# Attention block on one core: four-head score batches in a ring of three bank pairs, and one score bank in seven exponentiated on VectorE

## The chip, the cores and the metric

One core of one Trainium2 chip. The metric is device time in microseconds (us) of the core, the median over the runs named; lower is better. The kernel before takes 1316.6 us (two runs, 1308.5 and 1324.7). Every run also reports the mean clock that TensorE was granted, as a share of its full clock; runs more than 1.5% above the fastest of the same kernel are called slow and are left out of ratios.

## The reference

A transformer block in bf16 for 2048 tokens of width 640: multi-query attention (32 query heads of 20 dimensions, one head of keys and values), then a gated GELU feed-forward part of width 1536.

```python
def block(x, wq, wk, wv, wo, w_gate, w_up, w_down):       # x: 1 x 2048 x 640
    n = layernorm(x)
    q = (n @ wq).reshape(B, S, 32, 20).transpose(0, 2, 1, 3)
    k, v = n @ wk, n @ wv                                  # one head of 20, shared
    scores = einsum("bhqd,bkd->bhqk", q, k) * 20 ** -0.5
    o = einsum("bhqk,bkd->bhqd", softmax(scores), v)
    h = x + o.transpose(0, 2, 1, 3).reshape(B, S, 640) @ wo
    m = layernorm(h)
    return h + (gelu(m @ w_gate, approximate=True) * (m @ w_up)) @ w_down
```

The costly thing is the softmax: 32 x 2048 x 2048 exponentials. As 128 partitions that is 2048 PSUM banks of 128x512 fp32 scores.

## The kernel before

The heads have only 20 dimensions, so four of them lie on top of each other in the 128 rows of the TensorE array, 32 rows each. A "unit" is 128 keys x 512 columns (four head groups x 128 queries). Scores of two heads are computed into a pair of banks by two matmuls over 32 rows each, ScalarE exponentiates the pair (128x1024) into SBUF, and once four heads are done, four matmuls of 32 columns each multiply by the values. Keys lie in the partitions, so no transposition is needed; a column of ones in `v_ext` gives the softmax denominators.

The kernel divides PSUM into eight banks. Before: two pairs for scores, one bank for the value products, three for everything else (projections, feed-forward).

```python
A_BANKS = [0, 2]          # pairs: banks 0,1 and 2,3
V_BANKS = [4]
M_BANKS = [5, 6, 7]
...
def qk_source(e_name):
    ...
    nu = 2                                    # two heads in a batch
    tile = Tile(pA)                           # one bank pair
    ...
    def fn(e):
        for i, u in enumerate(range(u0, u0 + nu)):
            s, r, t, hf, kt = unit_info(u)
            ins = e.matmul(
                bank(A_BANKS[tile.slot] + i), kT4[32 * r:32 * r + 32, kt * P:(kt + 1) * P],
                qT[32 * r:32 * r + 32, (t // 4) % 2, 4 * hf:4 * hf + 4, (t % 4) * P:(t % 4) * P + P],
                start=True, stop=True, tile_position=(32 * r, 0))
        return ins
    o = Op("pe", fn, 300, deps, prio=-1000 + 0 * u0, acq=[tile], name=f"qk{u0}")
    ...
        ex = pl.add(Op("act", lambda e: e.activation(pa_sb[:, pt.slot, :], bank(A_BANKS[tile.slot], 2), ACT.Exp, scale=SM),
                       928, (o_,), prio=-1000, acq=[pt], name=f"exp{u0}"))
...
def make_pv(s):
    ...
        for r in range(4):
            _, pt, off = us[r]
            ins = e.matmul(bank(V_BANKS[vt.slot])[32 * r:32 * r + 32, :], v_ext[:, kt, :], pa_sb[:, pt.slot, off:off + 512],
                           start=(kt == 0), stop=(kt == NKT - 1), tile_position=(0, 32 * r))
```

The kernel is not written as loops. Each operation gets a planned duration and priority; a planner lays them out in time as the program is built and so fixes the order in which every engine gets its instructions. One that is late can then hold up those that stand behind it on its engine (in g2 below, 28.3 us of ScalarE).

The softmax here doesn't subtract the row's maximum and nothing guards it: scores larger than these inputs give would overflow.

## Time and profile before

| kernel before | value |
|---|---|
| time | 1316.6 us |
| mean granted clock of TensorE | 0.63 |
| busy: TensorE / ScalarE / VectorE / GpSimd | 88% / 77% / 17% / 20% |
| ScalarE waits for score matmuls | 248.0 us, 290 times |
| first exponential starts / last one ends | 16.25 / 1276.4 us |

The totals, the clock row, the chain of waits and the group of exponentials stand in the prediction below, with their reading. In the middle part, from 400 to 1260 us, the view by stretches says (columns: stretch and length, then busy time and count of TensorE, weight loads, VectorE, ScalarE and GpSimd, the granted clock, DMA share, GB/s):

```profile
400.00:1260.00 860.00, 774.93 (x3930) 219.55 (x3969) 121.44 (x257) 687.06 (x729) 189.06 (x204) 0.62 0.05 12
```

ScalarE is busy for 687 of 860 us here, at a clock of 0.62.

### The profile page before, as it was taken

The numbers are of one execution on the slowest core, as the hardware profiler recorded it, in microseconds if no ns is written. First come the engines' busy times: TensorE is split into PE (matmuls) and PEld (weight loads), VectorE is DVE, ScalarE is ACT, GpSimd is POOL, SyncE is SP. The second block draws the span as 40 slices with busy tenths as digits, with TensorE's granted clock in tenths as the row PEclk, the third lists the DMA queues.
The fourth block names the chain that finished last, engine by engine and source line by source line (L and its number), as shares of the span: only waits on it lengthen the run. The fifth ranks groups of instructions, "written<-read, shape, count | busy, mean of one in ns | idle before, by whom it ended". The sixth has DMA issues, their size and how long they took to land.

```text
span 1315.5 us, 14670 instructions
## 1 busy us (share of the span) xinstructions
PE 1160.0 (88%) x6129; PEld 342.5 (26%) x6188; DVE 220.3 (17%) x529; ACT 1018.0 (77%) x1081; POOL 266.0 (20%) x294
## 2 busy tenths in 40 slices
PE   5788888999997889989998888989999888999997
PEld 3311112222222222222222222222222222222245
DVE  6401010111112111021101211111010111111115
ACT  5598978788789876788767997688877898677861
POOL 3000001222013310223103221023211222013241
PEclk7755566655569765575556876576556766555669
DMA  5620000000000000000000000000000000000000
GB/s 147 146 103 14 9 14 9 9 15 2 18 14 14 9 9 11 14 14 9 9 13 13 14 9 14 19 1 13 9 14 19 10 14 1 18 14 9 14 0 21
DMA packets 47273, 27.33 MB, mean 21 GB/s; under 512 B 34408, under 2 KB 41960, under 8 KB 47208
## 3 DMA queue, kind: packets, MB, share of 16 engines
q1 hardware_dynamic: 47208, 26.40, 7.8%
q8 instruction: 48, 0.79, 0.2%
q14 instruction: 17, 0.14, 0.0%
HBM read 18.34 MB, written 2.88 MB: 16 GB/s over the span
## 4 chain that ended last, share of the span: by engine, by line
PE 53%; ACT 34%; DMA 5%; SPq 2%; DVE 2%; issue 2%; POOL 1%
ACT pa_sb L688 33%; PE ps L673 18%; PE ps L867 12%; PE ps L721 9%; PE ps L923 7%; PE ps L795 4%; PE ps L590 3%; SPq L410 2%; DMA rL<-lscr 1%; DMA lcol<-osb 1%; DMA lscr<-lrec 1%; POOL onT L769 1%; ACT th L890 1%; DMA xnT<-xn 1%; POOL sq L883 1%
## 5 line engine op out<-in xcount | busy, mean ns | idle before, releaser
L688 ACT ACTIVATE pa_sb<-ps 128x1024 bf16<-128x1024 f32 x1024 | 988.0, 1031 | 254.4 <-PE ps L673 248.0
L673 PE MATMUL ps<-qT,kT 32*128 32x512 bf16 x2048 | 545.2, 537 | 100.0 <-ACT pa_sb L688 87.7
L721 PE MATMUL ps<-pa_sb,v_ext 128*32 128x512 bf16 x2048 | 281.5, 541 | 3.5 <-ACT pa_sb L688 3.5
L673 PEld LDWEIGHTS ps<-qT,kT 32*128 32x128 bf16 x2048 | 102.3, 97 | 532.9 <-ACT pa_sb L688 413.8
L769 POOL TENSOR_TENSOR onT<-osb,rL 128x512 bf16<-128x512 f32 x31 | 39.2, 1264 | 555.2 <-DMA rL<-lscr 555.2
L867 PE MATMUL ps<-xnT,wg 128*128 128x256 bf16 (+1 forms) x540 | 113.0, 371 | 0.0
L923 PE MATMUL ps<-wd,hh 128*128 128x128 bf16 (+1 forms) x370 | 105.8, 419 | 5.7 <-issue 3.3
L721 PEld LDWEIGHTS ps<-pa_sb,v_ext 128*32 128x32 bf16 x2048 | 55.4, 98 | 192.7 <-issue 183.3
L883 POOL TENSOR_TENSOR sq<-gs 128x512 bf16<-128x512 bf16 x45 | 46.7, 1038 | 265.8 <-DVE gs L422 265.8
L867 PE MATMUL ps<-xnT,wu 128*128 128x256 bf16 (+1 forms) x540 | 94.5, 326 | 3.4 <-POOL sq L883 3.4
L422 DVE CAST gs<-ps 128x512 bf16<-128x512 f32 x45 | 31.1, 691 | 324.4 <-PE ps L867 324.4
L795 PE MATMUL ps<-wo_pad,onT 128*128 128x128 bf16 (+1 forms) x231 | 61.7, 386 | 16.5 <-POOL onT L769 8.4
L867 PEld LDWEIGHTS ps<-xnT,wg 128*128 128x128 bf16 x540 | 57.0, 128 | 53.2 <-issue 37.5
L867 PEld LDWEIGHTS ps<-xnT,wu 128*128 128x128 bf16 x540 | 51.3, 116 | 45.3 <-issue 24.4
L590 PE MATMUL ps<-xnT,wq_pad 128*128 128x512 bf16 (+1 forms) x140 | 51.2, 478 | 4.9 <-issue 4.9
L895 POOL TENSOR_TENSOR hg<-th,gs 128x512 bf16<-128x512 bf16 x45 | 52.1, 1159 | 3.7
L887 POOL TENSOR_TENSOR zz<-sq,gs 128x512 bf16<-128x512 bf16 x45 | 51.8, 1151 | 3.6
L904 DVE TENSOR_TENSOR hh<-hg,ps 128x512 bf16<-128x512 bf16 x48 | 32.3, 673 | 103.7 <-POOL hg L895 98.0
L893 POOL TENSOR_SCALAR th<-th 128x512 bf16<-128x512 bf16 x45 | 27.8, 617 | 86.6 <-ACT th L890 86.6
L744 DVE COPY osb<-ps 128x512 f32<-128x512 f32 x32 | 22.1, 691 | 133.7 <-PE ps L721 133.7
L923 PEld LDWEIGHTS ps<-wd,hh 128*128 128x128 bf16 x384 | 30.1, 116 | 53.8 <-issue 43.7
L422 DVE CAST qT<-ps 128x512 bf16<-128x512 f32 (+1 forms) x33 | 21.5, 654 | 126.1 <-PE ps L590 124.0
(66 smaller groups left out, 280.3 us busy)
## 6 DMA issues: line engine op xcount, KB each, us to landing
rL<-lscr SPq DMA_DIRECT2D x124, 64.0 KB, 2.0
out_dram<-xh SPq DMA_DIRECT2D x16, 160.0 KB, 1.8
lcol<-osb SPq DMA_DIRECT2D x124, 2.0 KB, 1.7
xh<-in_A_x_dram SPq DMA_DIRECT2D x6, 320.0 KB, 6.3
wg<-in_B_w_gate_dram SPq DMA_DIRECT2D x1, 1920.0 KB, 7.6
wu<-in_B_w_up_dram SPq DMA_DIRECT2D x1, 1920.0 KB, 13.1
wd<-in_B_w_down_dram SPq DMA_DIRECT2D x1, 1920.0 KB, 17.8
wq_st<-in_A_wq_dram SPq DMA_DIRECT2D x2, 400.0 KB, 4.4
```

The source lines that it names most:

```text
L422: return e.tensor_copy(o_ap(), i_ap())
L590: ins = e.matmul(bank(M_BANKS[mt.slot])[:, 0:n], wq_pad[:, c, g, :], xnT[:, c, tok], start=(c == 0), stop=(c == ND - 1))
L673: ins = e.matmul(bank(A_BANKS[tile.slot] + i), kT4[32 * r:32 * r + 32, kt * P:(kt + 1) * P], qT[32 * r:32 * r + 32, (t // 4) % 2, 4 * hf:4 ...
L688: ex = pl.add(Op("act", lambda e: e.activation(pa_sb[:, pt.slot, :], bank(A_BANKS[tile.slot], 2), ACT.Exp, scale=SM), 928, (o_,), prio=-10 ...
L721: ins = e.matmul(bank(V_BANKS[vt.slot])[32 * r:32 * r + 32, :], v_ext[:, kt, :], pa_sb[:, pt.slot, off:off + 512], start=(kt == 0), stop=( ...
L769: mu = op("pool", lambda e: e.tensor_tensor(onT[:, nt_.slot, 4 * hf:4 * hf + 4, :].rearrange("p g n -> p (g n)"), osb[:, ot.slot, :], rL[: ...
L795: ins = e.matmul(bank(M_BANKS[tl_.slot])[:, 0:c1 - c0], onT[:, nt_.slot, g, :], wo_pad[:, g, c0:c1], start=(g == 0), stop=(g == NG - 1))
L867: ins = e.matmul(bank(M_BANKS[tl_.slot])[:, j * n:(j + 1) * n], w[:, c, fc * P:(fc + 1) * P], xnT[:, c, tok], start=(c == 0), stop=(c == N ...
L883: a1 = op(pE, (lambda gt, st_: lambda e: e.tensor_tensor(sq[:, st_.slot, :], gs[:, gt.slot, :], gs[:, gt.slot, :], ALU.mult))(gt, st_), tt ...
L887: a3 = op(pE, (lambda gt, st_, zt: lambda e: e.tensor_tensor(zz[:, zt.slot, :], sq[:, st_.slot, :], gs[:, gt.slot, :], ALU.mult))(gt, st_, ...
L895: a6 = op(pE, (lambda gt, tt, ht_: lambda e: e.tensor_tensor(hg[:, ht_.slot, :], th[:, tt.slot, :], gs[:, gt.slot, :], ALU.mult))(gt, tt, ...
L923: ins = e.matmul(bank(M_BANKS[tl_.slot])[:, 0:c1 - c0], hh[:, ht.slot, f, i * P:(i + 1) * P], wd[:, f, c0:c1], start=(f == 0), stop=(f == ...
```

## The change

Its intent: relieve both engines at once. All four heads' scores are computed together, since four matmuls of 32 rows fill the rows of the array, which halves their time; the score pairs become three, so that TensorE can run ahead; and where VectorE has room, the last bank of a batch is exponentiated there. That bit trick needs no table: scale and add so that the integer's upper bits are the exponent of a bf16 and its lower seven bits the fraction, then correct the fraction by a quadratic (`et` is C2·u + C1, times u, added to the integer), and read the 16 bits as bf16.

```diff
-    A_BANKS = [0, 2]
-    V_BANKS = [4]
-    M_BANKS = [5, 6, 7]
+    A_BANKS = [0, 2, 4]
+    V_BANKS = [6]
+    M_BANKS = [7]
...
-        nu = 2
-        tile = Tile(pA)
+        t1, t2 = Tile(pA), Tile(pA)
...
+            for r in range(4):
+                ins = e.matmul(
+                    bank(A_BANKS[(t1, t1, t2, t2)[r].slot] + r % 2), kT4[32 * r:32 * r + 32, kt * P:(kt + 1) * P],
+                    qT[32 * r:32 * r + 32, (t // 2) % NQ, 4 * hf:4 * hf + 4, (t % 2) * P:(t % 2) * P + P],
+                    start=True, stop=True, tile_position=(32 * r, 0))
...
+    def exp1(o_, tile):                       # ScalarE, one bank
+            ... e.activation(ps_sb[:, pt.slot, :], bank(A_BANKS[tile.slot]), ACT.Exp, scale=SM), 502
+    def exp_dve(o_, tile):                    # VectorE, the other bank of the pair
+        p1 = pl.add(Op("dve", lambda e: e.tensor_scalar(
+            ej[:, jt.slot, k * 512:(k + 1) * 512], bank(A_BANKS[tile.slot] + 1), EA, EB, ALU.mult, ALU.add), 690, ...
+        if k == 1:                            # the rest for two banks at a time
+            e2: tensor_scalar(eu[:], ej[:, jt.slot, :], 127, None, ALU.bitwise_and)                 430
+            e3: tensor_scalar(et[:], eu[:], C2, C1, ALU.mult, ALU.add)                              430
+            e4: tensor_tensor(et[:], et[:], eu[:], ALU.mult)                                        690
+            fin: tensor_tensor(pd_sb[:, pt.slot, :], ej[:, jt.slot, :], et[:], ALU.add)             690
...
+        use_d = dstate["tile"] is not None or (D_FROM <= s < NS - 6 and dve_backlog(o_.end) < D_BACKLOG)
```

The middle of this diff is condensed: four planned operations are written as one line each, with the planned ns at the end. Cut away are: queries projected for two tiles at a time instead of four, the memset of `wq_pad` moved from VectorE to GpSimd, the multiply by the up projection moved from VectorE to GpSimd (VectorE copies the projection out of PSUM instead), fewer and smaller feed-forward buffers, two pieces instead of one in the last normalisation, freed score banks handed to the projections after the last scores, and planner constants (a planned cost of 107 ns where TensorE changes its kind of matmul, and a rule that keeps other matmuls from starting when a score batch is about to be due).

## The prediction

> **What bounds the kernel now.** I read the engine totals first, then the clock row, the chain that ended last, the costly groups, and last the timelines of stretches where ScalarE waits.
>
> ```profile
> PE 1160.0 (88%) x6129; PEld 342.5 (26%) x6188; DVE 220.3 (17%) x529; ACT 1018.0 (77%) x1081; POOL 266.0 (20%) x294
> PEclk7755566655569765575556876576556766555669
> PE 53%; ACT 34%; DMA 5%; SPq 2%; DVE 2%; issue 2%; POOL 1%
> L688 ACT ACTIVATE pa_sb<-ps 128x1024 bf16<-128x1024 f32 x1024 | 988.0, 1031 | 254.4 <-PE ps L673 248.0
> ```
>
> The 1024 exponentials are the largest work of any engine but TensorE, and ScalarE waited 248 us for score matmuls (L673). So neither engine alone is the bound: TensorE is late, and it is late at a granted clock of 0.63. The chain says the same, 53% TensorE and 34% ScalarE.
>
> ```profile
> 548.00:551.40 3.40, 3.06 (x20) 0.64 (x16) 0.00 (x0) 3.40 (x4) 0.00 (x0) 0.50 0.00 0
> 551.40:554.80 3.40, 3.40 (x18) 1.34 (x14) 0.00 (x0) 2.15 (x3) 0.00 (x0) 0.50 0.00 0
> 554.80:558.20 3.40, 2.93 (x24) 1.19 (x25) 0.69 (x1) 2.98 (x4) 2.42 (x3) 0.99 0.00 0
> 565.00:568.40 3.40, 1.94 (x20) 0.56 (x16) 0.25 (x1) 3.40 (x5) 0.00 (x0) 1.00 0.03 2
> 568.40:571.80 3.40, 2.94 (x17) 0.92 (x17) 0.00 (x0) 3.22 (x4) 0.00 (x0) 0.52 0.23 62
> ```
>
> These are stretches with the busy times of PE, PEld, DVE, ACT and POOL, then the clock. The clock is 0.5 or 1.0, nothing between, and 0.5 comes with a PE that is busy throughout.
>
> ```profile
> 551.28 0.62 PE L721 MATMUL ps<-pa_sb,v_ext 128*32 128x512 bf16 x4
> 551.83 1.25 PE L867 MATMUL ps<-xnT,wg 128*128 128x256 bf16 x5
> 553.01 0.61 PE L673 MATMUL ps<-qT,kT 32*128 32x512 bf16 x2
> 553.55 1.25 PE L867 MATMUL ps<-xnT,wg 128*128 128x256 bf16 x5
> 554.73 0.45 PE L673 MATMUL ps<-qT,kT 32*128 32x512 bf16 x2
> 502.50 1.02 ACT L688 ACTIVATE pa_sb<-ps 128x1024 bf16<-128x1024 f32 x1 [0.48 <-PE ps L673]
> 504.56 1.02 ACT L688 ACTIVATE pa_sb<-ps 128x1024 bf16<-128x1024 f32 x1 [1.03 <-PE ps L673]
> ```
>
> Start to start, a batch of two score matmuls or of four value matmuls takes 0.54 us at the slow clock (551.28 to 551.83): 512 columns at 1.2 GHz are 427 ns, and 0.11 us more goes with each change of kind. ScalarE meanwhile stands still for 0.48 and 1.03 us in turn.
>
> **What the Trainium skill says.** "TensorE: Matmul & The Clock Gate", Part 1, has a clock of 4/8 or 8/8 set by activity in windows of 3413 ns. The trace agrees: its clock changes only on a 3.41 us grid, between 0.5 and 1.0. The page does not say how a partly used array counts, so I counted: per window, matmul columns times the share of the 128x128 array that they use (a two-head score batch counts half, a four-head value batch whole), over the 8192 cycles of full speed. Of 285 half-speed windows, a threshold of 0.375 sorts all but 10, and none above 0.375 stayed slow; of 100 full-speed windows, 0.35 sorts all but 5 (below it the clock falls). "TensorEngine Tiling (Array Packing)", Key Properties, says that a change of tiling mode drains the engine: that is the 0.11 us. "VectorE: DVE Perf Modes", the perf-mode tier table: 4x for tensor_scalar, 2x for tensor_tensor in bf16 SBUF, no more from PSUM than 2x. The trace has 0.29, 0.42 and (fp32 PSUM) 0.69 us for 512 columns, which fits. "SBUF — State Buffer", Who interferes with whom: a VectorE instruction in a 2-port mode or with two SBUF inputs and a GpSimd instruction shut each other out. One GpSimd multiply of the tail took 1.46 us instead of 1.15 beside such a VectorE multiply.
>
> **The change part by part.** *Scores.* 1024 two-head batches become 512 four-head ones, because four K=32 matmuls fit the rows together. Weighted columns stay the same; stream time falls. Columns in time: scores 524k to 262k, values 262k, all else 547k (counted in the order of instructions). That is 1333k before, 1071k after. Changes of kind fall from 1665 to 1104 (same count): 178 to 118 us. At the slow clock TensorE needed 1111+178 = 1289 us and will need 893+118 = 1011; at the full clock 556+178 = 734 and 446+118 = 564. For the kernel before at 0.63: 882+178 = 1060 of a 1260 us middle part.
>
> *Clock.* Before, attention alone at the slow clock, with no pause, counts 1024 weighted columns per three batches of 0.54 us = 1.61 us, or 0.27 of full: it can never lift the clock. After, two batches: 1024 in 1.07 us, 0.40, above 0.375. A saturated slow TensorE lifts its own clock within one window, so it can't stay the bound. Averaged over 950 us the array's share is 1071k/(2400 x 950) = 0.47, against 0.34 now. I expect a mean clock of 0.75 to 0.85, and TensorE at 446/0.8+118 = 675 us.
>
> *ScalarE.* Start to start, half of the exponentials follow within 0.90 to 0.94 us, so take 0.91 (the 1.02 of a record overlaps its neighbour). Now 732 of 1024 columns and 292 of 512 are left: 292 of 2048 banks go to VectorE, one in seven. One of 512 takes 0.91-0.427 = 0.483. So 732 x 0.91 + 292 x 0.483 = 666+141 = 807, and 42 tanh at 0.52 add 22: 829 us, against 932+22 before. So of the gain the arithmetic of one in seven is 125 us and the rest is waiting.
>
> *VectorE.* 292 scale-and-add from PSUM at 0.69 = 201 us; per pair of banks, two tensor_scalar of 1024 columns (0.29 + 0.13 = 0.42 each) and two tensor_tensor (0.42 + 0.27 = 0.69 each): 146 x 2.22 = 324. Sum 525. The 48 copies of the up projection add 33, the multiply that left for GpSimd takes away 28: 220 to about 755 us. The lock: GpSimd works about 315 us (266 + 42 x 1.15), a third of the time; an instruction that meets one waits some 0.5 us, so 584 x 0.18 = 105 us more (an estimate). VectorE then has about 830 us in the middle part: as full as ScalarE.
>
> *Buffers.* Score pairs 2 to 3, but each batch takes two, so the next batch starts when the first of its predecessor's pairs has been read, and must be done in the 0.91 us of the second (0.483 where VectorE shares it). It needs some 0.65 us slow, 0.44 fast. So a shared batch at the slow clock costs about 0.17 us: 292 x 0.35 x 0.17 = 17 us. The other matmuls fall from three banks to one: some 24 uses per two tiles, 64 batches of 1.62 us, 4.3 us for each; filling takes 1.5 to 3 us, the copy another. Tight, but it holds.
>
> *Ends.* The first exponential starts at 16 us and the end comes 40 us after the last; after the last scores 49k columns follow instead of 61k. I take 16 and 36.
>
> *Sum.* Middle: 829, plus 15 for the start where keys arrive late (ScalarE is busy 30.5 us of 16 to 66), 17 for shared batches, 45 for bursts that begin at the slow clock (some 60 at 0.75), and 60 for VectorE and GpSimd running late in a fixed order: 966. With the ends, 1018; I say 1020.
>
> **The rivals.** *VectorE becomes the bound.* For it: 830 us with the lock, an order fixed ahead, and value matmuls that stand in front of scores in TensorE's queue and wait for VectorE's last step. If the bitwise step on uint16 runs without a fast mode (1.22 instead of 0.42), 146 x 0.8 = 117 us more: 1090. Against it: the bf16 rows at fast modes, and eight, five and three buffers between. *TensorE stays slow.* If four-row batches count no more than two-row ones, the clock stays near 0.6, TensorE needs 446/0.6+118 = 861, and at its present 84% that is 1025+52 = 1080. Against: the threshold sorts so well with weights by area. *The single bank for projections* delays the feed-forward part into the tail: 20 to 40 us more. Against: fewer columns after the last scores. *ScalarE alone*, everything hidden: 829+15+52 = 900; against: no stretch of this kernel has three engines near full without waits.
>
> **Range and chances.** The floor is 900, the two bad cases lie at 1080 to 1090, and most estimates at 990 to 1050. I take 965 to 1090. For less than 2% gain more than 270 us of the gain would have to vanish: 2%. Slower: 2%.
>
> **What would show it.** A mean clock over 0.72; score batches half as many at the same 0.54 or 0.32 us spacing; ScalarE's waits for scores well under 120 us and its share at 80 to 87%; VectorE at 70 to 85%, with fast steps at 0.42 and 0.69; GpSimd multiplies longer than 1.15 us. The prediction is wrong if the clock stays near 0.63, if the bitwise step takes over 1 us, or if value matmuls wait long for VectorE.

## The result, and the profile after

The changed kernel takes 1045.22 us (median of 1043.35 and 1047.09, both fast). A ratio in this document is the mean time of one kernel's fast runs over that of the kernel before's fast runs of the same rounds, so it is not quite the ratio of the medians quoted. Here it is 0.794 (95% interval 0.772 to 0.816): 20.6% less time. The result is correct. In a later session, on another chip, the same kernel gave 1038.24 us over six runs, ratio 0.791 (0.787 to 0.796).

Engine totals, clock row, shares of the chain that ended last, and the groups that matter, of the changed kernel (groups: line, engine, operation, output<-input, shape and count, then busy us and mean ns of one, then idle time before them and what ended most of it):

```profile
PE 739.6 (71%) x6314; PEld 281.4 (27%) x6348; DVE 782.7 (75%) x1425; ACT 883.2 (84%) x1081; POOL 343.5 (33%) x322
...
PEclk9565655787797877998888887997789897998998
...
ACT 34%; PE 33%; DVE 30%; issue 3%; DMA 0%; POOL 0%; SPq 0%; DVEq 0%
...
L739 ACT ACTIVATE pa_sb<-ps 128x1024 bf16<-128x1024 f32 x732 | 712.2, 1029 | 117.5 <-PE ps L723 106.8
...
L748 ACT ACTIVATE ps_sb<-ps 128x512 bf16<-128x512 f32 x292 | 175.0, 599 | 0.5 <-PE ps L723 0.5
...
L762 DVE TENSOR_SCALAR ej<-ps 128x512 uint16<-128x512 f32 x292 | 201.1, 689 | 166.5 <-PE ps L723 164.7
...
L777 DVE TENSOR_TENSOR pd_sb<-ej,et 128x1024 uint16<-128x1024 uint16 x146 | 120.8, 827 | 1.8
...
L776 DVE TENSOR_TENSOR et<-et,eu 128x1024 bf16<-128x1024 bf16 x146 | 120.0, 822 | 2.0
...
L773 DVE TENSOR_SCALAR eu<-ej 128x1024 uint16<-128x1024 uint16 x146 | 85.6, 586 | 2.2
...
L775 DVE TENSOR_SCALAR et<-eu 128x1024 bf16<-128x1024 uint16 x146 | 81.0, 555 | 2.0
```

TensorE has fallen from 88% to 71%, and the clock row, which had 5 and 6 in most slices, has 7 to 9 from the eighth slice on; in the first seven it is mostly 5 and 6 still. The exponentials of ScalarE are 732 pairs and 292 single banks instead of 1024 pairs, and it waits 106.8 us for scores instead of 248.0. But the chain that ended last is now shared by three engines in nearly equal parts, 34, 33 and 30%. The same stretch view of the middle part, shorter now:

```profile
400.00:1000.00 600.00, 432.07 (x3714) 158.23 (x3732) 475.52 (x809) 539.62 (x666) 230.98 (x210) 0.86 0.07 16
```

ScalarE works for 540 of 600 us, at a clock of 0.86. The start of the kernel is different. From 66 to 183 us no feed-forward matmul has run yet (the first of the changed kernel is at 198.9 us), so that TensorE has little but attention to do. The kernel before, then the changed one:

```profile
66.00:183.00 117.00, 100.83 (x478) 20.83 (x485) 10.52 (x23) 102.50 (x110) 5.61 (x5) 0.58 0.12 37
```

```profile
66.00:183.00 117.00, 79.77 (x596) 22.22 (x598) 75.74 (x139) 103.48 (x126) 6.23 (x5) 0.61 0.05 12
```

The four-head batches leave the clock at 0.61 here, where it was 0.58. Of what the engines wait for, these lines matter (waiter, line, what it waited for; us in total, times, longest):

```profile
ACT pa_sb L739 <- PE ps L723: 106.8, 153, 8.1
PEld ps L723 <- DVE ej L762: 89.9, 82, 1.8
PEld ps L834 <- DVE pd_sb L777: 70.5, 75, 3.6
```

The second and third are new: weight loads of score batches (L723) wait for the VectorE step that frees the shared bank, and value matmuls (L834) for VectorE's last step. TensorE works in a fixed order, so each of these can hold up the next scores too. VectorE itself is late for a visible reason. The first two lines below are the views of one line's instructions each (ns: minimum/median/maximum), the fence after them a piece of the timeline (start us, duration us, engine, line, operation):

```profile
L773 DVE TENSOR_SCALAR eu<-ej x146: 375/427/1497, 63.3 to 1000.0; 128x1024 uint16<-128x1024 uint16 x146
...
L777 DVE TENSOR_TENSOR pd_sb<-ej,et x146: 636/691/1685, 66.6 to 1002.1; 128x1024 uint16<-128x1024 uint16 x146
```

```profile
604.32 1.15 POOL L1009 TENSOR_TENSOR ft<-ft,gs 128x512 bf16<-128x512 bf16 x1
604.49 1.27 DVE L773 TENSOR_SCALAR eu<-ej 128x1024 uint16<-128x1024 uint16 x1
...
606.84 1.15 POOL L1019 TENSOR_TENSOR hh<-ft,us 128x512 bf16<-128x512 bf16 x1
606.87 1.40 DVE L775 TENSOR_SCALAR et<-eu 128x1024 bf16<-128x1024 uint16 x1
```

The bitwise step has a median of 427 ns and goes up to 1497. At 604.49 it starts while a GpSimd multiply is running (604.32 to 605.47) and takes 1.27 us: the multiply's remaining 0.98 us and then about 0.3 of its own. That is a lock, not a slower rate. The step at 606.87 fares the same: the multiply from 606.84 ends at 607.99, and the step ends at 608.27, again 0.3 us later.

At the start, the memset of `wq_pad` went from VectorE to GpSimd. The group of it before, then after:

```profile
L453 DVE MEMSET wq_pad<- 128x2560 uint32 x1 | 2.2, 2192 | 1.3 <-PEq L1005 1.3
```

```profile
L486 POOL MEMSET wq_pad<- 128x5120 bf16 x1 | 4.4, 4365 | 0.0
```

It takes twice as long and ScalarE, which writes the query weights into `wq_pad`, starts at 5.74 us instead of 3.60. The first exponential starts at 19.3 instead of 16.25 us.

### The profile page after: what moved, and what is told of

Read it like the earlier page. It is cut to its first block, busy times and chain, and to the rows that moved or that the text cites. A ratio compares the mean times of both kernels' runs of the same rounds, so it can differ in the third digit from the quotient of the medians.

```text
span 1045.3 us, 16159 instructions
## 1 busy us (share of the span) xinstructions
PE 739.6 (71%) x6314; PEld 281.4 (27%) x6348; DVE 782.7 (75%) x1425; ACT 883.2 (84%) x1081; POOL 343.5 (33%) x322
## 4 chain that ended last, share of the span: by engine, by line
ACT 34%; PE 33%; DVE 30%; issue 3%; DMA 0%; POOL 0%; SPq 0%; DVEq 0%
ACT pa_sb L739 31%; PE ps L723 12%; PE ps L834 9%; DVE ej L762 6%; PE ps L984 5%; DVE et L776 4%; DVE pd_sb L777 4%; DVE eu L773 4%; DVE et L775 3%; ACT ps_sb L748 2%; PE ps L911 2%; PE ps L624 2%; PE ps L1038 2%; DVE us L455 1%; DVE gs L455 1%
## 5 line engine op out<-in xcount | busy, mean ns | idle before, releaser
L739 ACT ACTIVATE pa_sb<-ps 128x1024 bf16<-128x1024 f32 x732 | 712.2, 1029 | 117.5 <-PE ps L723 106.8
L723 PE MATMUL ps<-qT,kT 32*128 32x512 bf16 x2048 | 238.6, 454 | 198.0 <-ACT pa_sb L739 153.2
L762 DVE TENSOR_SCALAR ej<-ps 128x512 uint16<-128x512 f32 x292 | 201.1, 689 | 166.5 <-PE ps L723 164.7
L834 PE MATMUL ps<-pa_sb,v_ext 128*32 128x512 bf16 x1464 | 202.1, 474 | 50.7 <-DVE pd_sb L777 41.3
L748 ACT ACTIVATE ps_sb<-ps 128x512 bf16<-128x512 f32 x292 | 175.0, 599 | 0.5 <-PE ps L723 0.5
L723 PEld LDWEIGHTS ps<-qT,kT 32*128 32x128 bf16 x2048 | 57.7, 93 | 398.8 <-ACT pa_sb L739 171.5
L884 POOL TENSOR_TENSOR onT<-osb,rL 128x512 bf16<-128x512 f32 x31 | 46.7, 1508 | 242.0 <-DMA rL<-lscr 241.7
L777 DVE TENSOR_TENSOR pd_sb<-ej,et 128x1024 uint16<-128x1024 uint16 x146 | 120.8, 827 | 1.8
L776 DVE TENSOR_TENSOR et<-et,eu 128x1024 bf16<-128x1024 bf16 x146 | 120.0, 822 | 2.0
L834 PE MATMUL ps<-ps_sb,v_ext 128*32 128x512 bf16 x292 | 118.4, 479 | 0.0
L834 PE MATMUL ps<-pd_sb,v_ext 128*32 128x512 bf16 x292 | 118.3, 478 | 0.0
L773 DVE TENSOR_SCALAR eu<-ej 128x1024 uint16<-128x1024 uint16 x146 | 85.6, 586 | 2.2
L834 PEld LDWEIGHTS ps<-pa_sb,v_ext 128*32 128x32 bf16 x1464 | 43.0, 103 | 156.4 <-DVE pd_sb L777 70.5
L775 DVE TENSOR_SCALAR et<-eu 128x1024 bf16<-128x1024 uint16 x146 | 81.0, 555 | 2.0
```

The lines of the kernel that those rows point to most:

```text
L723: ins = e.matmul(bank(A_BANKS[(t1, t1, t2, t2)[r].slot] + r % 2), kT4[32 * r:32 * r + 32, kt * P:(kt + 1) * P], qT[32 * r:32 * r + 32, (t ...
L748: ex = pl.add(Op("act", lambda e: e.activation(ps_sb[:, pt.slot, :], bank(A_BANKS[tile.slot]), ACT.Exp, scale=SM), 502, (o_,), prio=-1000, ...
L762: p1 = pl.add(Op("dve", lambda e: e.tensor_scalar(ej[:, jt.slot, k * 512:(k + 1) * 512], bank(A_BANKS[tile.slot] + 1), EA, EB, ALU.mult, A ...
L773: e2 = pl.add(Op("dve", lambda e: e.tensor_scalar(eu[:], ej[:, jt.slot, :], 127, None, ALU.bitwise_and), 430, firsts, prio=-950, acq=[ut], ...
L775: e3 = pl.add(Op("dve", lambda e: e.tensor_scalar(et[:], eu[:], C2, C1, ALU.mult, ALU.add), 430, (e2,), prio=-950, acq=[wt], name="e3"))
L776: e4 = pl.add(Op("dve", lambda e: e.tensor_tensor(et[:], et[:], eu[:], ALU.mult), 690, (e3, e2), prio=-950, name="e4"))
```

## The experiments

The gain is 271 us and as predicted in size, but the prediction tied it to particular parts. Theory: the four-head batch lifts the clock and removes most of the waiting, the share of VectorE brings 125 us less the costs. The rivals: other parts do it; or the lock or the planned durations limit it. All experiments but e3 are edits of the changed kernel. All give a correct result unless said otherwise. The rounds of one session share their runs of the kernel before, so ratios compare best. "Us from the ratio" means the ratio times 1318, the middle of the medians of the kernel before.

### e1: no share for VectorE

```diff
-    D_FROM, D_BACKLOG, SLACK = 14, 600.0, 100.0
+    D_FROM, D_BACKLOG, SLACK = 1000000, 600.0, 100.0
```

> The changed kernel with all exponentials left on ScalarE; four-head batches and the ring of three stay. Theory (two gains that add: TensorE no longer late through four-head batches, and 125 us of ScalarE's work moved): ScalarE needs 1024 x 0.91 + 22 = 954 us in the middle, with some 100 us of waits and 55 us of ends about 1110 us (1070 to 1140), clock 0.7 or more, ScalarE's share over 90%. Rival A (VectorE's share is what brought the gain, the four-head batches little): over 1230 us. Rival B (VectorE's lateness eats what it takes over): under 1065 us.

Measured: 1080.71 us, ratio 0.819 (0.814 to 0.825), clock 0.807. Totals and one line of the waits:

```profile
PE 800.3 (74%) x6348; PEld 278.2 (26%) x6348; DVE 233.5 (22%) x549; ACT 978.2 (91%) x1081; POOL 304.1 (28%) x322
```

```profile
ACT pa_sb L739 <- PE ps L723: 58.7, 60, 8.1
```

Without the share, ScalarE is 91% busy and clearly the bound; its wait for scores is 58.7 us, little more than half of what it is with the share. So the share takes 125 us of work off ScalarE and gives most of it back as waiting: 0.819 - 0.791 is 37 us. Where it gives it back is counted below, under "The waits". The clock doesn't need the share (0.807 without it).

### e2: two-head batches, share and ring kept

```diff
-        t1, t2 = Tile(pA), Tile(pA)
+        h2 = (state["u"] % 4) // 2
+        t1 = Tile(pA)
...
-            for r in range(4):
+            for r in (2 * h2, 2 * h2 + 1):
```

(and the bookkeeping for a batch of one pair)

> The changed kernel with scores in two-head batches of one bank pair each, ring of three and VectorE's share kept. Theory (the clock rises because four-head batches let attention alone pass 0.375 of the array): clock back to 0.55 to 0.68, score batches twice as many, TensorE again late, 1150 to 1230 us. Rival A (VectorE's share made the gain): 1040 to 1080 us.

Measured: 1071.96 us (the median of all four runs; of the three fast ones 1066.57), ratio 0.810 (0.802 to 0.818). The fast runs took 1062.85 to 1077.36 us at a clock of 0.777 to 0.799. The planner shared 270 banks instead of 292.

The theory failed here, and clearly: with two-head batches the clock was to fall back to 0.55 to 0.68 and the time to 1150 to 1230 us. The four-head batch brings 0.810 - 0.791, 24 us. It is not necessary for a high clock, and, as f3 will show, not sufficient either.

### e3: the kernel before, with scores over 64 rows

To test how a part-used array counts, the kernel before got score matmuls over 64 rows instead of 32: the same time and columns per matmul, twice the array. The result is wrong (two heads are summed).

```diff
-   bank(A_BANKS[tile.slot] + i), kT4[32 * r:32 * r + 32, kt * P:(kt + 1) * P],
-   qT[32 * r:32 * r + 32, ...], start=True, stop=True, tile_position=(32 * r, 0))
+   bank(A_BANKS[tile.slot] + i), kT4[64 * i:64 * i + 64, kt * P:(kt + 1) * P],
+   qT[64 * i:64 * i + 64, ...], start=True, stop=True, tile_position=(64 * i, 0))
```

> The kernel before with each score matmul over 64 rows instead of 32 (wrong result on purpose: it adds two heads), so that a two-head batch fills all rows for the same columns and the same number of instructions. Theory (the clock answers to columns times used share of the array): mean clock 0.63 to about 0.8, 1120 to 1200 us. Rival (it answers to busy time or to the number of matmuls): clock 0.63, 1305 to 1325 us.

Measured: 1156.68 us, ratio 0.876 (0.872 to 0.882), clock 0.863. Totals and clock row:

```profile
PE 925.7 (80%) x6188; PEld 309.1 (27%) x6188; DVE 219.8 (19%) x529; ACT 994.4 (86%) x1081; POOL 265.5 (23%) x294
...
PEclk9776698898799988988888978989779987988889
```

Nothing but the number of rows differs (and the values of the scores), and the clock goes from 0.63 to 0.86. So the clock counts the rows of the array in use, as the prediction had it; that it counts the columns too, and so the area, rests on the sorting of windows alone. The clock alone is worth some 163 us to the kernel before ((1 - 0.876) x 1318).

### e4: GpSimd's multiplies cut short

The GpSimd instructions of the activation (three multiplies, two scale-and-adds for a unit) work on 32 of 512 columns; the last multiply stays whole. The order and number of instructions stay. The feed-forward values are wrong, by less than the comparison's tolerance.

```diff
+            cut = slice(0, 512 if nt == 1 else 32)
...
-            a1 = op(pE, ... e.tensor_tensor(F(tt), G(gt), G(gt), ALU.mult) ...
+            a1 = op(pE, ... e.tensor_tensor(F(tt)[:, cut], G(gt)[:, cut], G(gt)[:, cut], ALU.mult) ...
```

> The changed kernel with the GpSimd multiplies of the activation cut to 32 of 512 columns, except the last one of each unit (wrong result on purpose); order and all else the same. Theory (the lock between VectorE and GpSimd costs on the path): VectorE's two-input steps fall from 0.82 to below 0.75 and its tensor_scalar steps from 0.57 to below 0.50 us, VectorE's busy time by 40 to 70 us, the time by 15 to 40 us. Rival (the lock is hidden): VectorE's busy time falls as much, the time by less than 6 us.

Measured: 1002.75 us, ratio 0.760 (0.755 to 0.765). A VectorE step, and ScalarE's wait for scores:

```profile
L773 DVE TENSOR_SCALAR eu<-ej 128x1024 uint16<-128x1024 uint16 x146 | 76.0, 520 | 2.2
```

```profile
ACT pa_sb L739 <- PE ps L723: 65.3, 109, 7.5
```

The step falls from 586 to 520 ns in the mean (the tensor_scalar steps were to come below 500; the other one did, at 445), ScalarE's wait from 106.8 to 65.3, and the kernel gains 0.791 - 0.760, about 42 us, a little over the 15 to 40 expected. It does not yet say whether the lock was the reason or the earlier end of GpSimd's work; g2 below is for that.

### f1: two-head batches, no share; the ring of three alone

Both edits of e1 and e2 together. What remains of the change is the ring of three pairs, with a single bank for projections, and the new planning.

> Two-head batches and no VectorE share: of the change only the ring of three pairs, the new order and the new feed-forward part stay. e1 and e2 left two of the gains standing together with the ring; this asks what the ring and order bring by themselves. Theory N (work that TensorE may start earlier packs its windows, lifts the clock, and that is most of the gain; each further part only shifts it): clock 0.70 to 0.80, 1080 to 1150 us. Rival (four-head batches and the share each bring over 100 us, whichever comes first): 1200 us or more, clock under 0.68.

Measured: 1170.12 us, ratio 0.889 (0.885 to 0.893), clock 0.722. The clock is in the range of the theory, the time is not: it lies between the theory's 1080 to 1150 and the rival's 1200. Still it is half of the gain, with neither four-head batches nor a share for VectorE. Its clock row:

```profile
PEclk9565557886596865877668875788658786577998
```

ScalarE waits 117.4 us for scores, against 248.0 in the kernel before.

### f2: the same, with two pairs and three projection banks

```diff
-    A_BANKS = [0, 2, 4]
+    A_BANKS = [0, 2]
...
-    M_BANKS = [7]
+    M_BANKS = [7, 4, 5]
```

> As f1, with the score ring back at two pairs and three banks for the projections as in the kernel before: what is left of the change is the order, the feed-forward part with its own copy of the up projection, and the tail. Theory R (the ring of three is what counts): back to 1230 to 1320 us, clock under 0.68. Rival (the new order alone does it): within 30 us of f1.

Measured: 1308.61 us, ratio 0.995 (0.989 to 1.001), clock 0.609. Its clock row:

```profile
PEclk9556555675565755686556565568555665575597
```

This is the kernel before in all that counts, and its time too: the new order, the feed-forward rework and the tail together are worth nothing that can be seen. So 0.995 - 0.889, some 140 us, come from the third pair (with the banks that it takes from the projections). Comparing the rows: 7 to 9 in 8 of the 40 slices (f2) and in 23 (f1). ScalarE's wait for scores, f2 and then f1:

```profile
ACT pa_sb L740 <- PE ps L724: 231.5, 343, 5.5
```

```profile
ACT pa_sb L740 <- PE ps L724: 117.4, 159, 7.9
```

### f3: four-head batches in a ring of two

The edits of f2's banks and of e1, with the four-head batch kept.

> Four-head batches, no share, a ring of two pairs: each batch needs both pairs empty, so ScalarE stands still for a batch's latency (0.44 us fast, 0.65 slow) every 1.82 us: 512 x 0.5 = 256 us on 954, with the ends about 1250 us (1190 to 1310). Rival (the third pair is not needed): within 25 us of e1, 1081 us.

Measured: 1452.76 us, ratio 1.103 (1.097 to 1.110), clock 0.683. The direction was the theory's; the size was outside its range of 1190 to 1310. A batch takes both pairs, so TensorE can't start the next scores until ScalarE has read the last of them. In the timeline:

```profile
699.96 1.94 ACT L739 ACTIVATE pa_sb<-ps 128x1024 bf16<-128x1024 f32 x2 [0.50 <-PE ps L723]
...
701.95 0.61 PE L723 MATMUL ps<-qT,kT 32*128 32x512 bf16 x4 [1.72 <-ACT pa_sb L739]
...
702.61 1.94 ACT L739 ACTIVATE pa_sb<-ps 128x1024 bf16<-128x1024 f32 x2 [0.72 <-PE ps L723]
```

The scores start as the exponentials end, and ScalarE stands still for 0.72 us until they are there: 2.65 us for a batch (699.96 to 702.61), where the pair of exponentials needs 1.82. That is 0.83 us a batch where 0.5 was expected, and 512 x 0.83 is 425 us. The clock of 0.683 is under the 0.722 of f1: the four-head batch alone doesn't make it high. It is good only together with the third pair.

### f4: true durations in the plan

The planner believes VectorE's steps to take 430, 430, 690 and 690 ns, while the means are 586, 555, 822 and 827. With true numbers the order should fit better.

```diff
-  fin 690, e2 430, e3 430, e4 690
+  fin 825, e2 590, e3 560, e4 825
```

> The changed kernel with the order planned on the step times that the trace shows beside GpSimd (0.59, 0.56, 0.825, 0.825 us instead of 0.43, 0.43, 0.69, 0.69); 244 banks instead of 292 go to VectorE. Theory (VectorE runs later than planned, and value matmuls and score pairs wait for it): waits fall by more than the 48 x 0.427 = 20 us of exponentials that go back to ScalarE, 1010 to 1035 us. Rival (lateness is not planned away, the share counts): 1050 to 1065 us.

Measured: 1051.52 us, ratio 0.799 (0.795 to 0.802). The theory failed. With longer steps in the plan fewer banks fitted (244 instead of 292), which gives 20 us of exponentials back to ScalarE. The time grew by some 10 us (0.799 - 0.791), so the better forecast won back about half of that, and not more than all of it.

### g1: the changed kernel again

> The changed kernel as it is, for the comparison with the other three on the same chip: 1040 to 1055 us, ratio to before 0.79 to 0.80.

Measured: 1038.24 us (1037.59 to 1040.08, six runs), ratio 0.791 (0.787 to 0.796), clock 0.838: a little under the range, and the reference for the differences above and below, since it has the narrow interval.

### g2: e4 plus filler work on GpSimd

As e4, and after each unit GpSimd runs five scratch instructions of 464 columns. The orders of TensorE, VectorE and ScalarE are those of e4, as the two traces confirm; only GpSimd's work differs.

```diff
+   dum[0] = op("pool", dm, 0.0, (a7, m_dz, dum[0]), -5000, name="dummy")   # five instructions on dz, dy
```

> As e4 (short multiplies on GpSimd, wrong on purpose), with five idle GpSimd instructions of 464 columns on scratch tiles after each unit, which nobody waits for; the order on TensorE, VectorE and ScalarE is the same. GpSimd is as full as in the changed kernel, its chain short. Theory (the lock is what e4 removed): VectorE's steps back to about 0.57 and 0.82 us, ratio back to 0.785 to 0.80 (1035 to 1050 us). Rival (the length of GpSimd's chain delayed the feed-forward matmuls): ratio stays at 0.755 to 0.77 (about 1003 us).

Measured: 1055.11 us, ratio 0.804 (0.800 to 0.808). The same VectorE step, and a wait that came with the fillers:

```profile
L777 DVE TENSOR_SCALAR eu<-ej 128x1024 uint16<-128x1024 uint16 x146 | 80.8, 553 | 2.2
```

```profile
ACT ft L1013 <- POOL ft L1012: 28.3, 18, 3.0
```

The steps are long again (553, 589, 804 and 808 ns), although the fillers compute nothing that anyone waits for. The time is more than back, over the 1035 to 1050 expected. The fillers overshoot: GpSimd is busy for 396 us, where it is 341 in g1. And 28.3 us are ScalarE's tanh waiting for GpSimd work that stands behind fillers, which the fillers caused by their place and not by the lock. Taking all of it off gives an estimate of 1027, against 1003 for e4; by the ratios (0.804 - 0.760, 58 us, less 28) it is 30 us. So that GpSimd's being busy makes the steps longer is shown; what it costs the whole kernel is some 25 to 30 of the 42 us by this run, an estimate.

### g3 and g4: less work on GpSimd, correct

g3 takes one of GpSimd's multiplies away: VectorE, when it copies the up projection out of PSUM, multiplies it by the gate at once. g4 does the same and moves the square of the gate to VectorE as well.

```diff
-   a6 = op(pE, ... e.tensor_tensor(F(tt), F(tt), G(gt), ALU.mult) ...
-   e2 = evac("dve", us[:, ut.slot, :], tbank(um), ...)
+   e2 = op("dve", ... e.tensor_tensor(us[:, ut.slot, :], tbank(um), G(gt), ALU.mult) ...
```

and in g4 also

```diff
-   a1 = op(pE, ... e.tensor_tensor(F(tt), G(gt), G(gt), ALU.mult) ... tt_d
+   a1 = op("dve", ... e.tensor_tensor(F(tt), G(gt), G(gt), ALU.mult) ... 430
```

> A right version with one GpSimd multiply less per unit: VectorE multiplies the up projection by the gate as it copies it out of PSUM (0.69 us as before), so GpSimd needs no multiply of its own for it. GpSimd's busy time falls by 42 x 1.34 = 56 us. Theory (lock): a third of e4's gain, ratio 0.775 to 0.788 (1020 to 1037 us). Rival: no change, 0.79 to 0.80.

> As g3, and the square of the gate on VectorE (42 x 0.42 = 18 us more there, 42 x 1.19 = 50 us less on GpSimd). Theory (lock): another 5 to 15 us below g3. Rival (VectorE is the fuller engine and pays for it): as g3 or up to 15 us above.

Measured, g3: 1039.66 us, ratio 0.791 (0.787 to 0.796): no gain, the theory missed. GpSimd fell from 341 to 283 us and the planner placed 282 shared banks. g4: 1021.92 us, ratio 0.778 (0.774 to 0.782), clock 0.84. Its totals:

```profile
PE 726.7 (71%) x6348; PEld 276.1 (27%) x6348; DVE 728.7 (71%) x1419; ACT 888.0 (87%) x1081; POOL 233.5 (23%) x238
```

GpSimd is down to 233.5 us and VectorE to 728.7, although it took over work: its steps are 463, 498, 771 and 765 ns now, and the planner shared 278 banks, 14 fewer than in g1, which alone takes some 27 us off VectorE (an estimate: 14 times 0.69, and 7 times the four steps' sum). By its ratio g4 gains 17 us over g1 (0.791 - 0.778). Why g3 gained nothing and g4 did is not settled. This is the best correct version, faster than both kernels.

### What could not be tried

The ring of three pairs alone in the kernel before: with a single bank for projections its planner gets stuck and no program is built (the planner stops with 137 operations open, feed-forward matmuls of the last tiles among them). f1 and f2 stand in for it, in the changed kernel's planning. They change the score pairs and the projection banks together, so "the ring" here means both. A share for VectorE with a ring of two was not run.

## Why the prediction was right, and which of its steps failed

The prediction was 1020 us, range 965 to 1090; it came to 1045.22. The end was right, and so were most sizes. But the largest step of its reasoning named the wrong part, and in the sum of its waits one term was far too small and the others too large, so that the close hit is in part luck.

The runs, in us from the ratio:

| score batch | ring | share | run | us |
|---|---|---|---|---|
| two heads | 2 | no | f2 | 1311 |
| two heads | 3 | no | f1 | 1171 |
| four heads | 2 | no | f3 | 1454 |
| four heads | 3 | no | e1 | 1080 |
| two heads | 3 | yes | e2 | 1067 |
| four heads | 3 | yes | g1 | 1043 |

- **Clock, the rule: right.** The count of array area above 0.375 of a window was made on the kernel before alone. Made again over the traces of the runs (my own count over the matmul records), it sorted the half-speed windows of the changed kernel with 3 misses in 114, of e1 with 1 in 122, of e3 with 3 in 95, of f1 with 1 in 190 and, the worst, of f2 with 13 in 300. e3 changed only the rows and moved the clock from 0.63 to 0.86. Expected for the changed kernel: 0.75 to 0.85; measured 0.814 and 0.825, and 0.86 in the middle.
- **Clock, the cause: wrong.** This is the step that failed. The prediction said of the two-head batch that "it can never lift the clock", and gave the lift to the four-head batch. That sentence holds for attention alone with a saturated slow TensorE, but the kernel never is that alone: projections and feed-forward matmuls count whole. f1 lifts the clock from 0.609 to 0.722 with two-head batches, and e2 to 0.78 to 0.80. What they share is the third pair. And f3, with four-head batches in a ring of two, has only 0.683; the changed kernel itself, while attention runs nearly alone (66 to 183 us), only 0.61. The prediction's 0.40 of the array takes a TensorE with no pause; there it is busy for 80 of 117 us. The mean area in use, by the same count, went from 0.335 of full speed in f2 to 0.377 in f1, 0.417 in e1 and 0.422 in the changed kernel. A plausible reading, argued and not shown: with two pairs a burst of other matmuls at the slow clock makes ScalarE wait, which spreads the same columns over more time and keeps the windows under the threshold; with three pairs TensorE has a pair in hand, the waits fall (231.5 to 117.4 us), the columns close up, and the windows pass it.
- **The ring: counted only as a cost.** The prediction's "Buffers" gave it 17 us of loss (which is real and larger, see "The waits"). It is worth 140 us beside two-head batches, and without it the four-head batch loses 143 (f3 against f2). Half of the whole gain comes from a part that the prediction named only as a cost.
- **The share: its arithmetic right, its worth not.** ScalarE's floor was to be 829 us: 732 pairs and 292 single banks are what ran, and 43 of the 48 tanh fall before the last exponential. From start to start a pair takes 0.908 us in the median, and a single bank 0.48 where a tanh follows at once. Against the 954 of before that is 125 us less. But e1 shows a gain of 37 us beside four-head batches. Beside two-head batches the share is worth 104 us. The two parts overlap: each is large in the ring of three without the other (91 and 104) and small beside it (24 and 37). The prediction added them up.
- **The waits: the sum nearly right, its terms not.** From the first exponential at 19.3 to the end of the last at 1010.1 us is 991; less the floor, 162 us of waiting, where 15 + 17 + 45 + 60 = 137 was predicted. This is nearly all of the 27 us by which the time exceeds the unrounded sum of 1018; the start came 3 us late (19.3 for 16), the tail was 1 us shorter (35.2 for 36). But the terms miss by more, and cancel. Counted over the starts of ScalarE's instructions in the trace (what each took beyond 0.908, 0.483 or 0.52 us until the next one started): up to 66 us 17 us, where 15 were predicted; after shared banks 91 us, where 17 were predicted; all the rest some 55, where 45 + 60 stood. After 265 of the 277 shared banks that a pair follows, ScalarE waits for the next scores: 0.18 us in the median where those run at the full clock, 0.43 at the half one, where the prediction had 0 and 0.17. Its batch times were right (0.45 and 0.66 us from the start of the scores to the exponential, for 0.44 and 0.65). What it left out, as a reading: a pair's banks are free only at the end of its record, 1.03 us and not 0.91 after its start. In e1 the waits after 66 us are 57 us, with the share 145: the 88 us between are what the share gives back of its 125, and nearly all of it follows the shared banks.
- **VectorE's steps: right.** Medians 427, 427, 691 and 691 ns, where 0.42, 0.42, 0.69 and 0.69 us were predicted, and 689 for the step from PSUM. The rival of a slow bitwise step is out.
- **The lock: right in kind, 105 us predicted, 81 by the means less the medians.** The means stand above the medians by 159, 128, 131 and 136 ns, 146 times each: 146 x 0.554. That the one that comes second is blocked and not slowed, as the prediction took it from the Trainium skill ("SBUF — State Buffer", Who interferes with whom), is what the step at 604.49 shows. GpSimd pays too: its multiply of attention outputs takes 1508 ns in the mean instead of 1264. Cutting GpSimd's work brought 42 us (e4), of which the lock has perhaps 25 to 30 (g2).
- **VectorE's load:** 782.7 us busy, with the lock in it, where 755 + 105 were expected (its terms add up to 750). The shared work is 201 + 407 of it; all else is 174 us, not the 230 assumed. It isn't the bound, but at 30% of the chain it is no longer beside the path.
- **The single bank for projections "holds":** the feed-forward part was not pushed into the tail, which is 35.2 us, where it was 39.1 before. The rival of 20 to 40 us more is out.

Two of its readings were loose. It says that the clock of 0.5 comes with a PE busy throughout, but its own lines have 3.06 of 3.40 us busy at 0.50 and 2.93 at 0.99. And ScalarE's pauses of 0.48 and 1.03 us are of another stretch (502 us) than the matmuls above them (551 us).

Of its signs, the clock (over 0.72), ScalarE's share (84%), VectorE's (75%) and the longer GpSimd multiplies came as named. Two were borderline: ScalarE's waits for scores were to be "well under 120" and came to 106.8, and value matmuls do wait for VectorE, 70.5 us in the weight loads.

## What to carry to other kernels

Where two engines wait for each other in turn, count first how far the producer may run ahead: one more buffer pair was worth more here (140 us) than halving the time of the scores after it (91 us), and the halved work was a loss without it. Don't add up the gains of parts that cure the same wait; build the kernel with each part alone and with each left out. Work moved to an idle engine is worth its arithmetic only if that engine's lateness can't hold up the bound, so look at whom it shares ports with before it is given more. And a step of the consumer that gets shorter leaves the producer less time for the next batch: here 91 of the 125 us taken off ScalarE came back as waits just behind the shortened steps.

## What the Trainium skill lacked or had wrong

- "TensorE: Matmul & The Clock Gate", Part 1, gives windows of 3413 ns and a clock of half or whole, which every trace here agrees with, but not how a partly used array counts. Here it counts by area: matmuls over 64 rows instead of 32, nothing else changed but the values of the scores, moved the mean clock from 0.63 to 0.86; columns times the used share of the array, with a threshold of 0.375 of a full-speed window, missed 3 of 114 half-speed windows of the changed kernel and 10 of 285 of the kernel before (a count made again, window by window, gave 3 of 119 and 12 of 288).
- "VectorE: DVE Perf Modes", the perf-mode tier table, has no row for bitwise operations and no column for 16-bit integers; no page was found with a time for one, though the skill's general conditions for the modes, which go by the size of an element, leave room for it. `bitwise_and` on uint16 in SBUF took 427 ns in the median for 1024 columns, the same as the multiply-and-add beside it.
- "SBUF — State Buffer", Who interferes with whom, has the rule of the lock, and the trace agrees; what it comes to in a kernel where both engines are used is not there. Here 584 VectorE instructions beside a GpSimd busy for a third of the span lost 139 ns each (means less medians), with single ones going from 427 to 1497 ns.
- No page was found that names GpSimd's time for a memset (a general rate of GpSimd for one element is given): 5120 bf16 columns took 4.37 us, and the same bytes as 2560 uint32 on VectorE 2.19 us.
